# Two transformer layers on one core: fixed load order, free PSUM banks for the first projections, PV placed behind scores, and a new order table

## The chip, the cores and the metric

The kernel runs on one core of one Trainium2 chip. The metric is the device time of one launch in microseconds (us). The engines that appear below are PE (TensorE, matrix multiply; its weight loads are listed apart as PEld), DVE (VectorE), ACT (ScalarE), POOL (GpSimd) and SP (SyncE, which only issues DMA transfers here). Every engine runs its own list of instructions in the order in which the program wrote it and waits for others by semaphores.

## The reference

The input is x, one sequence of 2048 tokens with 512 channels in bf16. Two layers are computed with the same weights. Each layer is a sliding-window attention followed by an MLP, both with a layer norm in front and a residual behind:

```
x = x + A(layernorm(x));  x = x + B(layernorm(x))      # this line twice

A: q, k, v = split(x @ wqkv)                # 32 heads of 16 channels
   s = q k^T / 4;  s = -1e9 where not 0 <= i - j < 256
   o = softmax(s) v;  return o @ wo
B: return gelu_tanh(x @ w1 + b1) @ w2 + b2  # 512 -> 1792 -> 512
```

A query sees its own key and the 255 before it. The layer norm has neither scale nor shift.

## The kernel before

**Tiles and stages.** x stays in SBUF as 16 tiles of 128 tokens (`X`). Two layers make 32 tiles, taken as 16 blocks of two tiles (256 tokens). For a block b the stages are:

- `lnq(b)`: for each tile statistics (`bn_stats`, L635), `rstd` on POOL (L642), the normalized tile `xn` (L645), a PE transpose (L36) and its copy to `xnTA` (L622 on DVE or L624 on ACT); then the Q projection in two groups of 512 columns, each for two of the four 128-channel chunks.
- `kv(b)`: the K projection in two such groups, each copied by DVE with a parity mask into `KT` (L712), and the V projection, one group a tile, copied into `Va`.
- `attention(b)`: nine or ten *visits*. A visit is one group of 16 or 24 small score matmuls (32 x 64 tiles of the PE array, 8 of them side by side) into four PSUM banks, followed by two exponentials on ACT (L800, 128 x 1024 each) into the ring buffer `E`. Masks (L823, DVE or POOL) cut the window's edges.
- PV: for each half of the heads (cp = 0, 1) two *phases* of 32 to 64 small matmuls each (64 x 17 tiles) multiply `E` by `Va` into two banks. The column of ones in `Va` yields the sum for the softmax. DVE transposes (`TT`, L886), takes the reciprocal (`Rc`), multiplies (`TM`, L891) and transposes back (`OT`, L896).
- `outproj`: the output projection, the residual (L677) and the second layer norm into `xnTB`.
- `mlp(J)`: ten jobs of two or four tiles. Some of the first product's groups go over DVE (bias, L957) and a gelu in place on ACT (L960), the others straight through gelu on ACT (L970). The second product ends in the residual, and in the second layer in the DMA to the output.

All matrix multiplies of the projections and the MLP use the whole 128 x 128 array. Every matmul goes through L32 and every PE transpose through L36, whatever the stage, so in the trace the tiles' names tell them apart.

**What sets the order.** The order of each engine's instructions is written by a planner (`_Plan`) while the program is built. Each piece of work is a node with an engine, a duration in ns that the planner assumes, what it reads and writes, and a priority; a lower number goes first. `run` steps through time, and whenever an engine is free, it takes the ready node with the lowest priority, provided that a PSUM bank is to be had. Priorities come from the block (200 per block) plus offsets by stage, such as 16 per visit, 80 * cp + 95 for PV, 110 for the Q projection two blocks ahead and 140 for K and V of the next block. To each priority a step from an *order table* is added: two long strings `TUNE`, of which one character stands for one class of node. The first string gives a step of the character's code minus 80 (P is 0, a character is between about -46 and +46), the second leans a node to its other engine.

For each node the planner also assumes a fixed time until its result is visible, a 94 ns cost when PE goes from one tile shape to another (`SWITCH`), and 1300 ns for a change of ACT's function table. The shapes have the letters f (whole array), r (scores) and c (PV).

**PSUM.** Eight banks are shared by classes: `sc` (four banks for a visit), `o` (bank 6 or 7, for all projections and transposes), `od` (two banks for PV) and `m1` (any one bank, for the first MLP product).

**Loads.** SP issues twelve loads from one queue. `load` is called in the order x tiles 0-1, Wqkv part 0 (Q), part 1 (K), x tiles 2-3, Wqkv part 2 (V), b1, x tiles 4-7, Wo, b2, W1, x tiles 8-15, W2. It gives each a planned issue time `i`, 480 ns after the one before, and a priority made from it:

```
dma(fn, writes, prio=-1000.0 + i / 1e3, dur=sp_t[1] - i, issue=issue)
```

Then `add` puts the table's step on that priority as on any other. The issue lines are L595 (x), L600 (Wqkv), L609 (b1), L611 (Wo), L612 (b2), L613 (W1) and L615 (W2).

Of the kernel before, what the change touches and what calls it, by code (L numbers as in the profile page):

```python
# [180 lines left out]
class _Plan:  # L181
# [5 lines left out]
    AFF = 0.0  # L187
# [9 lines left out]
    def add(self, eng, fn, dur, reads=(), writes=(), prio=0.0, alloc=None, free=(), after=(), geo=None, table=None,  # L197
            dma=False, alt=(), war=(), lock=False, joins=()):
# [20 lines left out]
        if free and eng == "dve":  # L219
# [5 lines left out]
            alts=((eng, fn, dur, 0.0),) + alt, key=k, done=False, behind=None,  # L225
            heavy=any(a[0] == "pool" and a[2] > 600.0 for a in ((eng, fn, dur),) + alt),
        ))
        return i

    def run(self):  # L230
# [15 lines left out]
        last_lock = {"dve": None, "pool": None}  # L246
        last_geo = None
# [22 lines left out]
        seq = n  # L270
        while left:
# [9 lines left out]
            for e in engs:  # L281
                while pend[e] and pend[e][0][0] <= t + 1e-9:
                    _, i = heapq.heappop(pend[e])
                    for a in nodes[i]["alts"]:
                        if a[0] == e:
                            heapq.heappush(ready[e], (nodes[i]["prio"] + a[3], i))
                if efree[e] > t + 1e-9 or not ready[e]:
                    continue
                skipped = []
                pick = best = None  # L290
                while ready[e]:
                    p, i = heapq.heappop(ready[e])
                    nd = nodes[i]
                    if nd["done"]:
                        continue
                    if best is not None and p > best[0] + self.AFF:
                        skipped.append((p, i))
                        break
                    if (e == "pool" and locked["dve"] + (self.TAIL["dve"] + self.WAKE["pool"] if nd["heavy"] else 0.0) > t + 1e-9) or (
                            e == "dve" and nd["lock"] and locked["pool"] > t + 1e-9):  # L300
                        skipped.append((p, i))
                        continue
                    if nd["alloc"] is not None and fit(nd["alloc"][0]) is None:
                        skipped.append((p, i))
                        continue
                    if best is None:
                        best = (p, i)
                        pick = i
                        if e != "pe" or nd["geo"] == last_geo:
                            break  # L310
                    elif nd["geo"] == last_geo:
                        skipped.append(best)
                        pick = i
                        break
                    else:
                        skipped.append((p, i))
                for s in skipped:
                    if s[1] != pick:
                        heapq.heappush(ready[e], s)
                if pick is None:  # L320
                    continue
                nd = nodes[pick]
# [68 lines left out]
def bass_interleave_layers__sliding_block__dense_activation_gelu__prompt_kernel(  # L391
# [46 lines left out]
    PVLAG = 1  # L438
    POOL_M = 1110.0
# [19 lines left out]
    with ExitStack() as kctx:  # L459
        S_ = _Sched(nc, kctx)  # L460

        def sb(name, shape, dtype=dt.bfloat16):
# [73 lines left out]
        }, TUNE)  # L536
        add = PL.add

# [65 lines left out]
        load_x(0, 2)  # L604
        load_qkv(0)
        load_qkv(1)
        load_x(2, 2)
# [12 lines left out]
        def evac(dst, src, n, reads, writes, prio, free=(), after=(), two=False, kind="", boot=False):  # L620

            return add("dve", lambda e, B: e.tensor_copy(dst(B), src(B)), 334 if two else d_psum(n),  # L622
                       reads=reads, writes=writes + ([] if free else reads), prio=prio, free=free, after=after,
                       alt=() if kind not in ACT_OK and not boot else (("act", lambda e, B: e.activation(dst(B), src(B), AF.Copy, scale=1.0), d_act(n), 0.0 if boot else ACT_H),))  # L624
# [3 lines left out]
        def layernorm(tau, layer, dst, dcol, dname, prio):  # L628
# [21 lines left out]
            def tr(e, B):  # L650
# [5 lines left out]
                alloc=("o", [(g, 1)]), geo="f", war=[dname])  # L656
# [23 lines left out]
        def lnq(b, prio):  # L680

            xs = b % 2
            for j in range(2):
                layernorm(2 * b + j, 0, xnTA[:, xs], j * P, "xa%d_%d" % (xs, j), prio)
            xr = ["xa%d_0" % xs, "xa%d_1" % xs]
# [12 lines left out]
        def proj(g, which, i, xs, xr, prio, war):  # L698
            for half in range(2):
# [351 lines left out]
```

## Time and profile before

| what | value |
|---|---|
| median of 3 runs | 494.89 us (493.67 to 494.89) |
| the profiled execution, whole | 499.72 us |
| its span, first to last instruction | 498.0 us |
| mean granted PE clock | 0.976 |
| busy: PE / ACT / DVE / POOL | 459.2 / 403.6 / 370.4 / 217.3 us |
| PE matmuls | 8897 |
| exponentials (L800) | 304, 1032 ns each, 290.2 us |
| HBM read / written | 8.00 / 2.10 MB |

A row of the trace in order of time has the start in us, the duration in us, the engine, the line, the operation, the tile written and the tiles read, the shapes, the count of merged instructions, and in brackets the idle time before and what ended it. The rows of stretches give each engine's busy time with its number of instructions, then the granted clock, the share of the DMA engines and their rate. Matmuls overlap, and their ends are modelled, so distances between starts are safer than single durations.

### The profile page before, as it was taken

How to read it: one execution, taken by the hardware profiler on the slowest of the kernel's cores; microseconds unless marked ns; L12 is line 12 of the kernel's file. 1: busy time of each engine (PE TensorE's matmuls, PEld its weight loads, DVE VectorE, ACT ScalarE, POOL GpSimd, SP SyncE). 2: the span in 40 equal slices, each digit the busy share in tenths (PEclk: the TensorE clock that was granted, in tenths of full speed). 3: DMA queues.
4: the chain of work that ended last, by engine and by line, in shares of the span. 5: the costliest groups of instructions: out<-in, count | busy, mean ns of one | idle time of the engine just before them, and what ended most of it. 6: DMA issues, size and time to landing. Idle time of an engine off the chain costs nothing.

```text
span 498.0 us, 19388 instructions
## 1 busy us (share of the span) xinstructions
PE 459.2 (92%) x8897; PEld 245.5 (49%) x8897; DVE 370.4 (74%) x749; ACT 403.6 (81%) x481; POOL 217.3 (44%) x245
## 2 busy tenths in 40 slices
PE   4389769989988999999999999999998999999897
PEld 2254446465543545545544554455544444544554
DVE  4089887788997858987999689886887858773541
ACT  1079989889897889998899988899897899868433
POOL 4039772723655344644387306453342534630020
PEclk9599899999998999999999999999999999999899
DMA  7910000000000000000000000000000000100010
GB/s 235 364 45 3 3 4 3 3 3 1 4 3 3 3 2 5 3 3 3 3 3 3 3 3 3 4 2 3 13 13 24 3 9 8 34 1 24 12 33 21
DMA packets 9117, 11.33 MB, mean 23 GB/s; under 512 B 460, under 2 KB 8524, under 8 KB 9036
## 3 DMA queue, kind: packets, MB, share of 16 engines
q1 hardware_dynamic: 9036, 10.10, 6.2%
q8 instruction: 69, 1.13, 1.0%
q14 instruction: 12, 0.10, 0.1%
HBM read 8.00 MB, written 2.10 MB: 20 GB/s over the span
## 4 chain that ended last, share of the span: by engine, by line
PE 79%; DVE 9%; ACT 4%; SPq 3%; issue 2%; DMA 2%; POOL 0%; POOLq 0%
PE ps L32 76%; ACT E L800 3%; PE ps L36 2%; DMA Wqkv_sb<-in_A_wqkv_dram 2%; DVE KT L712 2%; SPq L595 2%; DVE stat L635 1%; DVE TT L886 1%; DVE Va L622 1%; SPq L600 1%; DVE X L677 1%; POOL E L823 0%; DVE xnTA L622 0%; DVE TM L891 0%; SPq L613 0%
## 5 line engine op out<-in xcount | busy, mean ns | idle before, releaser
L800 ACT ACTIVATE E<-ps 128x1024 bf16<-128x1024 f32 x304 | 290.2, 1032 | 28.3 <-PE ps L32 26.3
L823 POOL TENSOR_TENSOR E<-E,mask 128x512 bf16<-128x512 bf16 (+1 forms) x123 | 133.3, 1097 | 121.7 <-ACT E L800 57.9
L32 PE MATMUL ps<-W_sb,gT 128*128 128x512 bf16 x448 | 116.9, 384 | 0.0
L32 PE MATMUL ps<-xnTB,W_sb 128*128 128x512 bf16 (+1 forms) x560 | 110.9, 340 | 1.9 <-ACT xnTB L624 0.9
L642 POOL TENSOR_TENSOR rstd<-veps,mhalf 128x1 f32<-128x1 f32 x64 | 37.4, 596 | 108.9 <-DVE veps L639 108.6
L32 PE MATMUL ps<-xnTA,Wqkv_sb 128*128 128x256 bf16 x512 | 71.8, 283 | 13.0 <-DMA Wqkv_sb<-in_A_wqkv_dram 12.7
L32 PEld LDWEIGHTS ps<-xnTB,W_sb 128*128 128x128 bf16 x560 | 51.6, 98 | 44.2 <-issue 3.3
L32 PE MATMUL ps<-QT,KT 32*64 32x320 bf16 (+4 forms) x2976 | 66.7, 260 | 7.1 <-issue 3.9
L677 DVE TENSOR_TENSOR X<-X,ps 128x512 bf16<-128x512 bf16 x64 | 43.7, 683 | 35.9 <-PE ps L32 34.9
L970 ACT ACTIVATE gT<-ps,b1T 128x512 bf16<-128x512 f32 (+1 forms) x92 | 49.7, 586 | 20.0 <-PE ps L32 19.9
L823 DVE TENSOR_TENSOR E<-E,mask 128x512 bf16<-128x512 bf16 (+1 forms) x137 | 56.6, 439 | 12.3 <-ACT E L800 11.8
L32 PEld LDWEIGHTS ps<-xnTA,Wqkv_sb 128*128 128x128 bf16 x512 | 47.5, 101 | 33.5 <-issue 16.2
L32 PEld LDWEIGHTS ps<-W_sb,gT 128*128 128x128 bf16 x448 | 39.4, 98 | 44.7 <-issue 7.4
L712 DVE TENSOR_TENSOR KT<-ps,parmask 128x1024 bf16<-128x1024 f32 x32 | 38.8, 1219 | 25.6 <-PE ps L32 25.2
L32 PE MATMUL ps<-E,Va 64*17 64x192 bf16 (+3 forms) x3872 | 49.4, 230 | 7.5 <-issue 5.2
L32 PEld LDWEIGHTS ps<-QT,KT 32*64 32x64 bf16 x2976 | 28.0, 104 | 53.4 <-ACT E L800 34.1
L32 PEld LDWEIGHTS ps<-E,Va 64*17 64x17 bf16 x3872 | 39.4, 85 | 23.6 <-issue 10.0
L886 DVE STREAM_TRANSPOSE TT<-ps 128x1024 f32<-128x1024 f32 x32 | 39.8, 1245 | 14.1 <-PE ps L32 13.7
L635 DVE BATCH_NORM_STATS2 stat<-X 128x6 f32<-128x512 bf16 x64 | 43.4, 684 | 1.2 <-DMA X<-in_A_x_dram 0.5
L930 POOL TENSOR_TENSOR X<-X,b2b 128x512 bf16<-128x512 bf16 x32 | 36.6, 1153 | 17.4 <-DVE E L823 8.8
L957 DVE TENSOR_SCALAR gT<-ps,b1T 128x512 bf16<-128x512 f32 (+1 forms) x48 | 32.0, 674 | 7.5 <-PE ps L32 6.6
L32 PE MATMUL ps<-Wqkv_sb,xnTA 128*128 128x512 bf16 x128 | 33.5, 381 | 0.8 <-DMA Wqkv_sb<-in_A_wqkv_dram 0.7
(48 smaller groups left out, 335.6 us busy)
## 6 DMA issues: line engine op xcount, KB each, us to landing
W_sb<-in_B_w_dram SPq DMA_DIRECT2D x2, 1792.0 KB, 13.5
out_dram<-X SPq DMA_DIRECT2D x16, 128.0 KB, 1.7
Wqkv_sb<-in_A_wqkv_dram SPq DMA_DIRECT2D x3, 512.0 KB, 10.5
X<-in_A_x_dram SPq DMA_DIRECT2D x1, 1024.0 KB, 13.1
X<-in_A_x_dram SPq DMA_DIRECT2D x2, 256.0 KB, 2.9
X<-in_A_x_dram SPq DMA_DIRECT2D x1, 512.0 KB, 10.7
Wo_sb<-in_A_wo_dram SPq DMA_DIRECT2D x1, 512.0 KB, 8.8
b2b<-in_B_b_dram SPq DMA_DIRECT2D x1, 128.0 KB, 6.7
```

Of the source, the lines that this page charges most:

```text
L32: return self.e.matmul(*a, **k)
L36: return self.e.transpose(*a, **k)
L635: add("dve", lambda e, B: e.bn_stats(stat6[:, k6, :], X[:, t, :]), 590, reads=["X%d" % t], writes=["st%d" % k6], prio=prio)
L642: add("pool", lambda e, B: e.tensor_tensor(out=rstd[:, k : k + 1], in0=veps[:, k : k + 1], in1=mhalf[:], op=ALU.pow), 535, reads=["ve%d" % ...
L677: add("dve", lambda e, B: e.tensor_tensor(out=X[:, t, :], in0=X[:, t, :], in1=ps[:, B[g][0], :], op=ALU.add), d_psum(512), reads=["X%d" % ...
L712: add("dve", lambda e, B, g=g, i=i: e.tensor_tensor(out=KT[:, kb, :, 2 * i : 2 * i + 2, :].rearrange("p a c q -> p a (c q)"), in0=ps[:, B[ ...
L800: last_exp[0] = add("act", lambda e, B, g_=g_, gi=gi: e.activation(E[:, 2 * gi : 2 * gi + 2, e0 : e0 + 512], ps[:, B[g_][0] : B[g_][0] + 2 ...
L823: op = lambda e, B, Ew=Ew, Mw=Mw: e.tensor_tensor(out=Ew, in0=Ew, in1=Mw, op=ALU.mult)
L886: add("dve", lambda e, B: e.transpose(TT[:, s].rearrange("p a c q d -> p (a c q d)"), ps[:, B[g][0] : B[g][0] + 2, :].rearrange("p a n -> ...
L930: add("pool", lambda e, B: e.tensor_tensor(out=X[:, t, :], in0=X[:, t, :], in1=b2b[:], op=ALU.add), 1110, reads=["X%d" % t, "b2b"], writes ...
L957: add("dve", lambda e, B, g=g, fc=fc: e.tensor_scalar(out=gT[:, fc, 0:M], in0=ps[:, B[g][0], 0:M], scalar1=b1T[:, fc : fc + 1], scalar2=No ...
L970: gelu_last[0] = add("act", lambda e, B, g=g, fc=fc: e.activation(gT[:, fc, 0:M], ps[:, B[g][0], 0:M], AF.Gelu_apprx_tanh, bias=b1T[:, fc ...
```

## The change

**Loads.** `load` uses `-1e5 + i` as the priority, so the loads lie 480 apart. The call for x tiles 2-3 moves ahead of the Wqkv parts.

**First projections.** The Q projection of blocks 0 and 1, and K and V of block 0, take their PSUM bank from class `m1` instead of `o`; the transposes of the first four tiles do so as well. Their priorities go from -60..-30 to -900 (Q of block 0), -890 (K), -880 (Q of block 1) and -350 (V), and the second channel pair of Q and K gets 400 more than the first.

**The planner's choice for PE.** The rule that took a node of the same shape among equal priorities is gone. For PE every ready node's priority now gets an offset by the last shape and its own (`TURN`): +100 from f to c, +10 from f to r, -100 from r to c, -60 from c to r. An argument `chain`, which could hold a node behind another, is added, but no call uses it.

**Early offsets.** For blocks 0, 1 and 2 the output projection gets -100, -80 and -50, and PV half of that.

**Constants.** Planned durations: PV phase 638 ns instead of 640, and 344 instead of 472 for the first block of a layer; TT +36, the reciprocal 260 instead of 130, TM on POOL 1110 instead of 1200, OT 630 instead of 600, copies on ACT +14.

**Order table.** Both strings are replaced. The instructions themselves, their shapes and their number by stage stay; which engine takes a node that has two may change, and so may the order of all five engines. The loop inside a PV phase is rewritten with the same matmuls in the same order.

```diff
-                            heapq.heappush(ready[e], (nodes[i]["prio"] + a[3], i))
+                            if e == "pe":
+                                ready[e].append((nodes[i]["prio"] + a[3], i))
+                            else:
+                                heapq.heappush(ready[e], (nodes[i]["prio"] + a[3], i))
...
+                elif e == "pe":
+                    best = None
+                    for p, i in ready[e]:
+                        nd = nodes[i]
+                        if nd["done"] or nd["chained"] or (nd["alloc"] is not None and fit(nd["alloc"][0]) is None):
+                            continue
+                        x = (p + self.TURN.get((last_geo, nd["geo"]), 0.0), i)
+                        if best is None or x < best:
+                            best = x
+                    if best is not None:
+                        pick = best[1]
...
+    EARLY = {0: -100.0, 1: -80.0, 2: -50.0}
...
+        TURN = {("f", "c"): 100.0, ("f", "r"): 10.0, ("r", "c"): -100.0, ("c", "r"): -60.0}
...
-            dma(fn, writes, prio=-1000.0 + i / 1e3, dur=sp_t[1] - i, issue=issue)
+            dma(fn, writes, prio=-1e5 + i, dur=sp_t[1] - i, issue=issue)
...
         load_x(0, 2)
+        load_x(2, 2)
         load_qkv(0)
         load_qkv(1)
-        load_x(2, 2)
         load_qkv(2)
...
-                alloc=("o", [(g, 1)]), geo="f", war=[dname])
+                alloc=("m1" if tau < 4 and not layer else "o", [(g, 1)]), geo="f", war=[dname])
...
-                proj(g, 0, i, xs, xr, prio, ["Q%d_%d" % (cb, 2 * i + c) for cb in cols for c in range(2)])
+                prio = base + pair[i]
+                proj(g, 0, i, xs, xr, prio, ["Q%d_%d" % (cb, 2 * i + c) for cb in cols for c in range(2)], "m1" if b < 2 else "o")
...
-                pr = prio + 80 * cp + 95
+                pr = prio + 80 * cp + 95 + EARLY.get(b, 0.0) / 2
...
-                    add("pe", fn, 640.0 if t0 else 472.0, reads=rd, writes=["ps:" + g, "pv%d_%d_%d" % (b, cp, phase)], prio=pr,
+                    add("pe", fn, 638.0 if t0 else 344.0, reads=rd, writes=["ps:" + g, "pv%d_%d_%d" % (b, cp, phase)], prio=pr,
...
-            pr = prio + 20 * NV + 40
+            pr = prio + 20 * NV + 40 + EARLY.get(b, 0.0)
...
-        lnq(0, -60)
-        kv(0, -50, -30)
-        lnq(1, -55)
+        lnq(0, -900, (0, 400))
+        kv(0, -890, -350, (0, 400))
+        lnq(1, -880, (0, 400))
```

More of the change, by code (lines that the diff above doesn't have):

```diff
@@ L246, in run @@
         last_lock = {"dve": None, "pool": None}
+        held = {e: None for e in engs}
+        for nd in nodes:
+            nd["chained"] = False
+        for nd in nodes:
+            if nd["then"] is not None:
+                nodes[nd["then"]]["chained"] = True
         last_geo = None
@@ L291, in run @@
[L291 to L312, printed above, removed]
+                pick = None
@@ new lines, in run @@
+                if held[e] is not None:
+                    if (held[e] in [x[1] for x in ready[e]]):
+                        pick = held[e]
+                elif e == "pe":
[9 more added lines that the diff above has]
+                        pick = best[1]
+                else:
+                    skipped = []
+                    while ready[e]:
+                        p, i = heapq.heappop(ready[e])
+                        nd = nodes[i]
+                        if nd["done"]:
+                            continue
+                        if (e == "pool" and locked["dve"] + (self.TAIL["dve"] + self.WAKE["pool"] if nd["heavy"] else 0.0) > t + 1e-9) or (
+                                e == "dve" and nd["lock"] and locked["pool"] > t + 1e-9):
+                            skipped.append((p, i))
+                            continue
@@ L313, in run @@
                         pick = i
                         break
[L315 to L319, printed above, removed]
+                    for x in skipped:
+                        heapq.heappush(ready[e], x)
                 if pick is None:
                     continue
+                if e == "pe":
+                    ready[e] = [x for x in ready[e] if x[1] != pick and not nodes[x[1]]["done"]]
+                    held[e] = nodes[pick]["then"]
@@ L847, in pv @@
                 npi = max(len(q) for q in seq)
-                for phase in range(2):
+                steps = [(phase, c) for phase in range(2) for c in (2 * cp, 2 * cp + 1)]
+                need = []
+                for phase, c in steps:
                     rd = []
@@ L851, in pv @@
                         for k, q_lo, q_hi, e0 in seq[half]:
[L852 to L855 removed]
+                            pos, n, vn = moving(k, 2 * c + (half ^ phase), e0, (q_hi - q_lo) * HK)
+                            rd += ["E%d%s" % (ch, x) for ch in chunks(pos, n) for x in "abd"] + [vn]
@@ L881, in fn @@
-                        return x
-                    add("pe", fn, 640.0 if t0 else 472.0, reads=rd, writes=["ps:" + g, "pv%d_%d_%d" % (b, cp, phase)], prio=pr,
+                        for c, pi in [(c, pi) for c in (2 * cp, 2 * cp + 1) for pi in range(npi)]:
+                            for half in range(2):
+                                if pi >= len(seq[half]):
+                                    continue
+                                k, q_lo, q_hi, e0 = seq[half][pi]
+                                par = half ^ phase
+                                rows = slice(HK * half, HK * half + HK)
+                                pos, n, _ = moving(k, 2 * c + par, e0, (q_hi - q_lo) * HK)
+                                e1 = pos % RING
+                                o = (c - 2 * cp) * 256 + q_lo * HK
+                                last = phase == 1 and c % 2 == 1 and pi == len(seq[half]) - 1
+                                cuts = [(e1, o, n)] if e1 + n <= RING else [(e1, o, RING - e1), (0, o + RING - e1, n - RING + e1)]
+                                for x1, o1, n1 in cuts:
+                                    for r in range(RG):
+                                        x = e.matmul(
+                                            ps[32 * r : 32 * r + VW, B[g][par], o1 : o1 + n1],
+                                            Va[rows, (2 * b + k) % VR, c * HC + 2 * r + par, :],
+                                            E[rows, r, x1 : x1 + n1],
+                                            start=phase == 0 and (par, r) not in opened,
+                                            stop=last and (x1, o1, n1) == cuts[-1], skip_group_check=True)
+                                        opened.add((par, r))
```

126 lines of the change are left out of this document (54 added, 72 removed).

## The prediction

> **What bounds the kernel now.** I read the page first, then the table by stretches, then the start in order of time. The page says which engine is the bound over the whole run:
>
> ```profile
> PE 459.2 (92%) x8897; PEld 245.5 (49%) x8897; DVE 370.4 (74%) x749; ACT 403.6 (81%) x481; POOL 217.3 (44%) x245
> ...
> PE   4389769989988999999999999999998999999897
> ...
> PE 79%; DVE 9%; ACT 4%; SPq 3%; issue 2%; DMA 2%; POOL 0%; POOLq 0%
> ```
>
> PE is busy 459.2 of 498.0 us and holds 79% of the chain of waits. Its holes are in the first six slices. The stretches (columns: PE, PEld, DVE, ACT, POOL busy, granted clock, DMA share, GB/s) put numbers on them:
>
> ```profile
> 0.00:10.00 10.00, 6.08 (x24) 2.52 (x24) 5.75 (x19) 1.88 (x2) 5.60 (x22) 1.00 0.69 201
> 10.00:20.00 10.00, 0.01 (x1) 0.04 (x2) 0.08 (x1) 0.00 (x0) 0.00 (x0) 0.61 1.06 375
> 20.00:30.00 10.00, 8.65 (x52) 5.88 (x52) 4.66 (x15) 3.58 (x6) 1.42 (x3) 0.71 0.71 225
> ...
> 40.00:50.00 10.00, 8.80 (x197) 4.88 (x190) 10.00 (x26) 9.20 (x12) 10.00 (x13) 1.00 0.01 2
> 50.00:60.00 10.00, 7.60 (x200) 4.62 (x199) 8.92 (x16) 9.71 (x12) 7.98 (x9) 0.83 0.01 3
> 60.00:70.00 10.00, 7.32 (x237) 4.22 (x235) 9.21 (x20) 9.25 (x11) 6.91 (x8) 1.00 0.01 3
> 70.00:80.00 10.00, 8.34 (x168) 6.11 (x168) 7.43 (x15) 8.96 (x13) 5.63 (x5) 1.00 0.01 2
> ...
> 100.00:150.00 50.00, 45.63 (x1070) 26.83 (x1069) 43.11 (x86) 46.46 (x57) 23.04 (x24) 1.00 0.01 3
> ...
> 200.00:250.00 50.00, 49.87 (x1089) 26.61 (x1094) 43.38 (x91) 45.19 (x52) 24.44 (x29) 1.00 0.01 3
> ```
>
> There are three regimes. From 10 to 20 us every engine stands still while DMA runs at 375 GB/s. From 40 to 80 us ScalarE (9.2, 9.7, 9.3, 9.0 of 10) sets the pace and PE has holes. Later PE is full: 49.87 of 50 from 200 us on. The start in order of time says why nothing runs:
>
> ```profile
> 0.79 0.95 SPq L595 DMA_DIRECT2D X<-in_A_x_dram  x2
> ...
> 2.29 0.43 SPq L615 DMA_DIRECT2D W_sb<-in_B_w_dram  x1
> ...
> 2.76 1.67 SPq L613 DMA_DIRECT2D W_sb<-in_B_w_dram  x1
> ...
> 4.48 4.80 SPq L600 DMA_DIRECT2D Wqkv_sb<-in_A_wqkv_dram  x1
> ...
> 7.35 0.42 DVE L622 COPY xnTA<-ps 128x512 bf16<-128x512 bf16 x1
> ...
> 9.15 0.93 DVE L645 TENSOR_SCALAR xn<-X,statmv,rstd 128x512 bf16<-128x512 bf16 x2 [0.31 <-POOL rstd L642]
> ...
> 19.99 5.28 PE L32 MATMUL ps<-xnTA,Wqkv_sb 128*128 128x256 bf16 x24 [12.68 <-DMA Wqkv_sb<-in_A_wqkv_dram]
> ...
> 26.45 1.28 DVE L635 BATCH_NORM_STATS2 stat<-X 128x6 f32<-128x512 bf16 x2
> ...
> 28.31 1.91 PE L32 MATMUL ps<-xnTA,Wqkv_sb 128*128 128x256 bf16 x16
> ...
> 30.15 0.42 PE L32 MATMUL ps<-QT,KT 32*64 32x320 bf16 x16
> ...
> 30.75 1.94 ACT L800 ACTIVATE E<-ps 128x1024 bf16<-128x1024 f32 x2
> ```
>
> The two MLP weights (L613, L615) stand ahead of the first 512 KB of Wqkv. The order table did this: the loads differ by 0.48 in priority per issue, and a character of the table shifts a load by up to tens. The operand of the first projection is ready at 7.35 + 0.42 = 7.8 us; the projection starts at 19.99 and the first exponential at 30.75.
>
> **Loads and first projections.** The new load priorities lie 480 apart, so the table cannot reorder them: x tiles 0-1, 2-3, then the three parts of Wqkv. Nothing is added to the SP queue; twelve load issues stay twelve, only their places move. The two small x transfers are already first. The page has size and time to landing of each issue:
>
> ```profile
> W_sb<-in_B_w_dram SPq DMA_DIRECT2D x2, 1792.0 KB, 13.5
> ...
> Wqkv_sb<-in_A_wqkv_dram SPq DMA_DIRECT2D x3, 512.0 KB, 10.5
> ...
> X<-in_A_x_dram SPq DMA_DIRECT2D x2, 256.0 KB, 2.9
> ```
>
> They land 2.9 us after their issue. The second is issued by 1.28 us (halfway through the 0.95) and lands near 4.2. Behind it 512 KB take 1.4 us at 375 GB/s or 2.6 at the first stretch's 201 GB/s: Wqkv part 0 lands between 5.6 and 6.8, ahead of the operand. The far bound is the 10.5 us row taken whole from an issue at 1.8, which gives 12.3; that is a transfer behind a full queue, so I stay with the near end. PE then resumes at 7.9 instead of 20.0, **12.1 us** earlier (7.7 at the far bound).
>
> The 24 matmuls at 19.99 take 5.28/24 = 0.220 us each, the 16 at 28.31 take 1.91/16 = 0.119. The granted clock between is 0.61 and 0.71, so the long pause is paid twice; without it these 24 cost 24 x 0.101 = **2.4 us** less. The Trainium skill ("TensorE: Matmul & The Clock Gate", Part 1) says an idle window of about 3.4 us puts the clock back to half rate; the trace's 0.61 agrees, and by that rule this gain is lost only if the weights land after 10.7 us.
>
> Then comes the split of the first projections into pairs: channel chunks 0-1 of Q0, K0 and Q1 come first, chunks 2-3 (400 later) and V (-350) behind. Before the first scores stand 24 matmuls of 256 columns instead of 40 and a V group. They may use any of eight PSUM banks instead of two, so no projection waits for an evacuation. Q0 and K0 end at 7.9 + 16 x 0.119 = 9.8; xn of tiles 2-3 ends at 9.15 + 0.93 = 10.1; transposes, one copy (0.42 on DVE), eight matmuls (1.0) and a copy bring the first scores to about 12.9 us, against 30.15: **-17.2 us** for these three steps together. Bounds: 12.3 if the last copy overlaps the chunk before it, 17.3 if Wqkv lands at the far bound (4.4 later), so -18 to -13. W1 and W2 (1792 KB each) are late next, for they now stand behind everything but part of x. Even at 201 GB/s all loads (7.8 MB by their sizes) are in by 40 us, and the first MLP matmul comes far behind that, near 57 after the shift:
>
> ```profile
> 73.98 0.28 PE L32 MATMUL ps<-xnTB,W_sb 128*128 128x256 bf16 x1 [0.90 <-ACT xnTB L624]
> ```
>
> So this move costs nothing, with 17 us of cover.
>
> **What DVE gives back.** Between 26.45 and 30 us DVE did four bn_stats of later tiles (two take 1.28, so about 2.7 us, and 1.2 us of their small operations by my estimate) while PE prepared its scores. That cover goes. DVE then was 10.00 of 10 busy from 40 to 50, so up to 3.9 us can come back as late K, Q and xn. ScalarE may take the early copies and later windows have slack (7.43 at 70-80). Bounds 0 to +3.9; I take the middle, **+2 us**.
>
> **PV behind scores.** Whether a change of tile shape costs time is read here (PE in order of time, one group a row):
>
> ```profile
> 1.23 5.63 PE L32 MATMUL ps<-gT 128*128 128x512 bf16 x16 [1.23 <-DVE gT L572]
> ...
> 160.85 1.47 PE L32 MATMUL ps<-xnTB,W_sb 128*128 128x512 bf16 x6
> 162.24 0.42 PE L32 MATMUL ps<-QT,KT 32*64 32x192 bf16 x16
> ...
> 165.15 4.49 PE L32 MATMUL ps<-xnTB,W_sb 128*128 128x512 bf16 x20
> 169.47 0.81 PE L32 MATMUL ps<-Wo_sb,OT 128*128 128x512 bf16 x3
> ...
> 488.76 6.21 PE L32 MATMUL ps<-W_sb,gT 128*128 128x512 bf16 x28
> ```
>
> Twenty dense matmuls take 169.47 - 165.15 = 4.32, 0.216 each. Six should take 1.30, but the scores start 1.39 after them: 0.09 us a change. Counted from the first PE row to the last (1.23 and 488.76), shapes change 396 times; 61 PV groups, of which only 10 come right behind scores and 39 stand alone between dense groups. The new offsets (dense to PV +100, scores to PV -100) make PE take PV after a visit. One change saved for each of the 39 is **-3.7 us**. The far end is -6, if each of 64 phases (two for each of 32 PV groups of banks) saves one; the other end 0, if PV waits for a visit and the TT transpose, OT and output projection behind it are late. PE has the dense queue as cover there. The PV durations in the planner move no work by themselves.
>
> This move puts more small instructions together, and the trace has a price for that:
>
> ```profile
> 376.06 0.80 PE L32 MATMUL ps<-E,Va 64*17 64x256 bf16 x64
> 376.79 0.40 PE L36 MATMUL ps<-ident,xn 128*128 128x128 bf16 x4
> 377.12 0.80 PE L32 MATMUL ps<-E,Va 64*17 64x256 bf16 x64
> 377.85 0.37 PE L32 MATMUL ps<-QT,KT 32*64 32x64 bf16 x15
> 379.70 0.37 PE L32 MATMUL ps<-QT,KT 32*64 32x320 bf16 x9 [1.48 <-issue]
> ```
>
> The waits in total (us, times, longest) and the page's instruction queue:
>
> ```profile
> PE ps L32 <- issue: 9.4, 8, 2.0
> ```
>
> ```profile
> q8 instruction: 69, 1.13, 1.0%
> ```
>
> After 147 matmuls with their weight loads (294 instructions in 2.2 us) PE stops 1.48 us inside a visit and waits for nothing but its own issue. Eight such pauses make 9.4 us. The 69 instruction packets match 2 x 8897 / 69 = 258 instructions each, so I read them as instruction fetch overtaken by a burst. A visit with one PV phase is (24 + 64) x 2 = 176 instructions, under 258, when dense work follows, which the zero offset after PV allows; both phases and two visits exceed it. I take **0**, with bounds -8 (all gone) and +8 (twice as many). The Trainium skill ("Runtime: NRT & Kernel Launch", Instruction fetch mechanics) calls crossing a 16 KiB boundary "mostly hidden"; by it this term and the slower rival below would be nothing, but the row contradicts it.
>
> **Earlier output projections, order table, constants.** Blocks 0-2 get PV 50, 40, 25 and output projections 100, 80, 50 earlier, so the first MLP starts sooner inside the stretch that ScalarE bounds. PE has 2.4 + 2.7 + 1.7 = 6.7 us of holes from 50 to 80; ScalarE is full there and gelu is its work too, so I count **-2 us** (0 to -5). The new table reorders everything else: from 200 us nothing is left to win, from 100 to 150 there are 4.4 us. I take 0, bounds -4 to +4.
>
> **Sum.** -17.2 + 2 - 3.7 + 0 - 2 + 0 = -20.9 us. The profiled execution took 499.7 us (span 498.0 and 1.7 around it, which nothing here touches), so 478.8 for its like; the median is 494.89, 4.8 less, so **about 474 us**.
>
> **Rivals.**
> - The start is won and partly lost again: DVE and ScalarE stay backed up to 80 us. For it: 10.00 and 9.20 of 10 at 40-50. Against: PE work, not DVE, fills the later 400 us. The 12.7 of the DMA wait are won, 3.9 come back in DVE and the holes of 50-80 grow by about 1: 494.9 - 7.8 = 487.
> - The plan fits the chip better throughout: pauses gone (-8), holes at 100-150 gone (-4). 474 - 12 = 462. For: the old plan assumed weights 13 us early. Against: PE is full from 200 on.
> - Slower: instruction fetch. At 1.6 us a pause, (between 1.48 and the longest, 2.0), the 20.9 us are eaten by 13 further pauses. If a pause hits one in three of the 64 PV phases, that is 21 pauses, 34 us, and 474 + 34 = 508. For: each long pause in the trace ends such a burst. Against: bursts of single phases stay under 258.
> - The loads do not come in the written order, or land no sooner: then the 12.7 us wait remains and only the shape changes and the fill, about 5 us, are left, near 490. Against: steps of 480 cannot be crossed by a character.
>
> **How the numbers follow.** Chances: forecast 0.62 (own range 467 to 482), start partly lost 0.15, better throughout 0.14, fetch pauses 0.05, loads not moved 0.04. Low 462 takes in about half of the better case, high 488 most of the partly lost one. Within 0.3% (1.5 us, about what a measurement can tell from no change) and slower come only from the fetch case and a fetch case mixed with loads that don't move: faster 0.93, same 0.02, slower 0.05.
>
> **What would show it.** The wait of 12.68 us for Wqkv should be gone; PE should resume by 9 us and the first L800 row stand near 13. The 10-20 stretch should show PE above 7 of 10 at clock 1.00. Groups of PV should follow scores, and "issue" before PE stay near 9 us. A first exponential after 18 us, or 20 us of issue pauses, would make the forecast wrong; so would PE holes of over 10 us between 30 and 80.

## The result, and the profile after

| | before | changed |
|---|---|---|
| median | 494.89 us (4 runs, 493.67 to 495.25) | 483.35 us (4 runs, 481.85 to 484.32) |
| ratio | | 0.977, 95% interval 0.974 to 0.980 |
| profiled span | 498.0 us | 482.6 us |

The change makes the kernel 11.5 us faster. The forecast was 474, 20.9 us faster: the direction and the range hold, the gain is little more than half of the one forecast. In the medians below, two of six runs of the loads alone and one of six of their repeat with x 8-15 moved up are left out, because they fell into a slower state of the chip.

The page of the changed kernel:

```profile
PE 446.3 (92%) x8807; PEld 246.2 (51%) x8897; DVE 367.3 (76%) x747; ACT 405.1 (84%) x481; POOL 221.6 (46%) x249
...
PE   8987899998889999999999999999999999999897
...
PEclk9997799999989999999999999999999999999999
...
PE 75%; DVE 9%; ACT 9%; issue 4%; DMA 1%; SPq 0%
```

The empty second slice is gone. The trace has 8807 of 8897 matmuls, so 90 records are missing. I read the many idle times of 0.16 us "issue" before a single dense matmul as such gaps: PE waits for issue 49 times here and 8 times in the first profile of before, which has every record. So busy PE can't be compared with before to a few us. The start in order of time, as it was shown of before:

```profile
0.78 0.95 SPq L611 DMA_DIRECT2D X<-in_A_x_dram  x2
...
1.78 1.56 SPq L616 DMA_DIRECT2D Wqkv_sb<-in_A_wqkv_dram  x3
...
8.45 0.23 PE L36 MATMUL ps<-ident,xn 128*128 128x128 bf16 x1 [0.60 <-DMA Wqkv_sb<-in_A_wqkv_dram]
...
9.20 0.83 PE L32 MATMUL ps<-xnTA,Wqkv_sb 128*128 128x256 bf16 x6 [0.52 <-DVE xnTA L638]
...
10.31 4.75 PE L32 MATMUL ps<-xnTA,Wqkv_sb 128*128 128x256 bf16 x42
...
15.11 1.67 PE L32 MATMUL ps<-Wqkv_sb,xnTA 128*128 128x512 bf16 x7
...
16.71 0.42 PE L32 MATMUL ps<-QT,KT 32*64 32x320 bf16 x16
...
17.32 2.90 ACT L821 ACTIVATE E<-ps 128x1024 bf16<-128x1024 f32 x3
```

The projections start at 9.20 us instead of 19.99, the scores at 16.71 instead of 30.15, the exponentials at 17.32 instead of 30.75. Ahead of the scores stand all 48 matmuls of 256 columns (6 and 42) and V, not 24. The stretches (columns as before) show where PE still has holes:

```profile
10.00:20.00 10.00, 9.78 (x113) 6.58 (x112) 8.86 (x23) 6.17 (x9) 2.13 (x4) 1.00 1.06 371
20.00:30.00 10.00, 8.51 (x152) 5.34 (x152) 8.97 (x25) 10.00 (x13) 6.18 (x7) 1.00 0.56 178
30.00:40.00 10.00, 7.50 (x207) 3.74 (x210) 9.63 (x23) 8.99 (x11) 10.00 (x11) 1.00 0.01 2
40.00:50.00 10.00, 9.15 (x179) 4.99 (x153) 7.83 (x14) 8.27 (x10) 6.29 (x9) 0.66 0.01 3
50.00:60.00 10.00, 7.81 (x228) 4.60 (x233) 7.02 (x17) 8.80 (x10) 7.07 (x8) 0.72 0.02 5
```

The 304 exponentials are the same in every version and come in the same order, so three times split each run: to the first exponential, from it to the start of the last, and from there to the end of the span. The first and the last start stand in the answer for the line of the exponential. Of the changed kernel (span 482.6):

```profile
L821 ACT ACTIVATE E<-ps x304: 1017/1024/1117, 17.3 to 441.8; 128x1024 bf16<-128x1024 f32 x152
```

Of the kernel before, profiled a second time (span 493.6, time 495.3 us, so nearer to its median than the first profile):

```profile
L800 ACT ACTIVATE E<-ps x304: 1018/1023/1138, 30.1 to 454.8; 128x1024 bf16<-128x1024 f32 x152
```

| profiled execution | to the first | first to last | last to end | span |
|---|---|---|---|---|
| before, first profile | 30.7 | 426.4 | 40.9 | 498.0 |
| before, second profile | 30.1 | 424.7 | 38.8 | 493.6 |
| changed | 17.3 | 424.5 | 40.8 | 482.6 |
| changed, second profile | 17.4 | 422.1 | 40.6 | 480.1 |

Against the second profile of before the start gives 12.8 us, the long middle 0.2, and the end takes 2.0 back. So the gain lies ahead of the first exponential; the middle differs by 2.4 us between the two profiles of the changed kernel alone.

### The profile page after: what moved, and what is told of

It is laid out like the page before. It is cut to its first block, busy times and chain, and to the rows that moved or that the text cites. A ratio compares the mean times of both kernels' runs of the same rounds, so it can differ in the third digit from the quotient of the medians.

```text
span 482.6 us, 19304 instructions
## 1 busy us (share of the span) xinstructions
PE 446.3 (92%) x8807; PEld 246.2 (51%) x8897; DVE 367.3 (76%) x747; ACT 405.1 (84%) x481; POOL 221.6 (46%) x249
## 4 chain that ended last, share of the span: by engine, by line
PE 75%; DVE 9%; ACT 9%; issue 4%; DMA 1%; SPq 0%
PE ps L32 72%; ACT E L821 6%; PE ps L36 3%; DVE KT L732 2%; ACT gT L993 2%; DVE stat L651 1%; DMA Wqkv_sb<-in_A_wqkv_dram 1%; DVE OT L919 1%; DVE gT L980 1%; DVE QT L638 1%; DVE X L693 1%; ACT gT L983 1%; DVE E L844 0%; DVE xnTA L638 0%; ACT Va L640 0%
## 5 line engine op out<-in xcount | busy, mean ns | idle before, releaser
L32 PE MATMUL ps<-W_sb,gT 128*128 128x512 bf16 x406 | 106.1, 380 | 4.4 <-issue 3.0
L32 PE MATMUL ps<-xnTB,W_sb 128*128 128x512 bf16 (+1 forms) x536 | 105.4, 336 | 4.2 <-issue 1.9
L32 PE MATMUL ps<-QT,KT 32*64 32x320 bf16 (+4 forms) x2976 | 67.4, 263 | 8.4 <-ACT E L821 4.2
L32 PEld LDWEIGHTS ps<-xnTB,W_sb 128*128 128x128 bf16 x560 | 51.5, 98 | 43.8 <-issue 3.6
L32 PE MATMUL ps<-xnTA,Wqkv_sb 128*128 128x256 bf16 x512 | 70.1, 281 | 1.5 <-DVE xnTA L638 0.8
L32 PEld LDWEIGHTS ps<-W_sb,gT 128*128 128x128 bf16 x448 | 39.9, 98 | 44.9 <-issue 5.4
L32 PE MATMUL ps<-E,Va 64*17 64x192 bf16 (+3 forms) x3872 | 50.3, 233 | 7.7 <-issue 3.7
L32 PEld LDWEIGHTS ps<-xnTA,Wqkv_sb 128*128 128x128 bf16 x512 | 47.7, 100 | 18.5 <-issue 3.2
L32 PEld LDWEIGHTS ps<-QT,KT 32*64 32x64 bf16 x2976 | 27.8, 104 | 56.9 <-ACT E L821 36.4
L32 PEld LDWEIGHTS ps<-E,Va 64*17 64x17 bf16 x3872 | 40.1, 86 | 22.0 <-issue 7.4
L32 PE MATMUL ps<-Wo_sb,OT 128*128 128x512 bf16 x120 | 30.9, 380 | 1.1 <-issue 0.6
```

The costliest lines, as they stand in the source:

```text
L32: return self.e.matmul(*a, **k)
```

## The experiments

**The loads alone, and the loads undone.** The kernel before keeps the planned order of PE, ACT, DVE and POOL; only the SP queue is rearranged behind the planner.

```diff
         order = PL.run()
+        first_loads = ["X0", "X2", "Wqkv0", "Wqkv1", "Wqkv2", "b1raw", "X4", "Wo", "b2b", "W1", "X8", "W2"]
+        sp_loads = {PL.nodes[i]["writes"][0]: i for i in order if PL.nodes[i]["eng"] == "sp" and not PL.nodes[i]["deps"]}
+        order = [sp_loads[n] for n in first_loads] + [i for i in order if i not in sp_loads.values()]
```

> The kernel before, with the order of PE, ACT, DVE and POOL exactly as its planner wrote it; only the twelve loads on the SP queue are put into the order of the changed kernel (x 0-3, three parts of Wqkv, b1, x 4-7, Wo, b2, W1, x 8-15, W2). Theory 1 (the whole gain is the start, and it comes from the loads alone): first exponential near 16 to 17.5 us instead of 30.75, every later part unchanged, median 480 to 484. Theory 2 (banks, PV rule and order table carry a good part): median 487 to 491.

The changed kernel gets the old order of loads by the same lines with

```diff
+        first_loads = ["X0", "X2", "b2b", "W2", "W1", "Wqkv0", "b1raw", "Wqkv1", "X8", "X4", "Wqkv2", "Wo"]
```

> The changed kernel with all its orders as planned, but the twelve loads on the SP queue in the order that the kernel before had (x 0-3, b2, W2, W1, Wqkv 0, b1, Wqkv 1, x 8-15, x 4-7, Wqkv 2, Wo). Theory 1: the gain is gone, first exponential at 29 to 32 us, median 493 to 499. Theory 2: 486 to 490, still clearly under the kernel before.

Measured: the loads alone take 482.9 us, ratio to before 0.971 (0.966 to 0.977), against 0.977 for the whole change. With the loads undone the change takes 496.6, ratio 1.002 (0.999 to 1.006). Theory 1 holds on both sides: the loads carry the whole gain, and everything else of the change is in sum worth nothing beside them. In the trace of the loads alone (span 481.4) the first exponential is earlier than in the changed kernel, and earlier than the 16 to 17.5 us expected, but the middle is longer:

```profile
L800 ACT ACTIVATE E<-ps x304: 1018/1023/1098, 15.1 to 442.5; 128x1024 bf16<-128x1024 f32 x152
```

442.5 - 15.1 = 427.4 against 424.7. In order of time, DVE, PE and ACT show the place:

```profile
22.64 0.69 DVE L635 BATCH_NORM_STATS2 stat<-X 128x6 f32<-128x512 bf16 x1 [2.94 <-DMA X<-in_A_x_dram]
23.25 0.67 DVE L622 CAST QT<-ps 128x512 bf16<-128x512 f32 x1
...
23.98 1.09 PE L32 MATMUL ps<-xnTA,Wqkv_sb 128*128 128x256 bf16 x8 [2.80 <-DVE QT L622]
...
25.72 1.94 ACT L800 ACTIVATE E<-ps 128x1024 bf16<-128x1024 f32 x2 [2.86 <-PE ps L32]
```

The old order of DVE reads x 8-15 early, because the old queue had it early; in the written order it comes behind W1 and lands at 22.6 us. Behind the waiting instruction stands a copy of Q; PE waits for that copy, ACT for PE.

**The kernel before, profiled again.**

> The kernel before, unchanged, profiled once more. Its first profile lasted 499.7 us against a median of 494.9. If the extra 4.8 us lie in the wait for the first weights, the first exponential comes near 26 us here with a time of 494 to 496; if they lie elsewhere (clock, fetch pauses), it stays at 30 to 31 and the rest is shorter.

495.3 us, first exponential at 30.1. So the extra time of the first profile was not the wait for weights. Of the 4.4 us between the spans 0.6 lie at the start. Most of the rest are pauses of PE over 0.3 us, 9.4 us in the first profile and 6.7 in the second; seven of the eight stand at the same instructions in both and last differently. The rows behind the two longest, of the first profile:

```profile
151.16 0.36 PE L32 MATMUL ps<-E,Va 64*17 64x192 bf16 x24 [2.00 <-issue]
...
462.37 0.50 PE L32 MATMUL ps<-E,Va 64*17 64x64 bf16 x37 [1.81 <-issue]
```

and of the second:

```profile
148.74 0.48 PE L32 MATMUL ps<-E,Va 64*17 64x192 bf16 x24 [0.91 <-issue]
...
459.62 0.49 PE L32 MATMUL ps<-E,Va 64*17 64x64 bf16 x37 [1.29 <-issue]
```

**The first projections really deferred.**

```diff
-        lnq(0, -900, (0, 400))
-        kv(0, -890, -350, (0, 400))
-        lnq(1, -880, (0, 400))
+        lnq(0, -900, (0, 940))
+        kv(0, -890, 50, (0, 940))
+        lnq(1, -880, (0, 950))
```

> The changed kernel, with the second channel pair of the first Q and K groups 940 to 950 behind the first instead of 400, and the first V at 50 instead of -350, so that they really stand behind the first visit in priority; everything is planned again with the same order table. First exponential expected near 13.5 to 14.5 us against 17.3. If what is won at the first exponential is kept to the end: median 479 to 481. If the later order, for which the table was not made, takes it back: 485 to 493.

490.7 us, ratio 0.987 (0.982 to 0.991). The first exponential came at 14.9, 2.4 us earlier than in the changed kernel, and the run was longer, by 7.3 us between the medians and by some 5 by the ratios: the second expectation. From first to last exponential it took 431.8 us instead of 424.5. The start of PE:

```profile
9.39 0.23 PE L36 MATMUL ps<-ident,xn 128*128 128x128 bf16 x1 [1.18 <-DMA Wqkv_sb<-in_A_wqkv_dram]
...
10.14 0.83 PE L32 MATMUL ps<-xnTA,Wqkv_sb 128*128 128x256 bf16 x6 [0.52 <-DVE xnTA L638]
...
11.26 2.13 PE L32 MATMUL ps<-xnTA,Wqkv_sb 128*128 128x256 bf16 x18
13.44 1.03 PE L32 MATMUL ps<-Wqkv_sb,xnTA 128*128 128x512 bf16 x4
14.39 0.42 PE L32 MATMUL ps<-QT,KT 32*64 32x320 bf16 x16
```

Five changed priorities let the planner write the queues anew: DVE has 738 instructions instead of 747, ACT 488 instead of 481. That the table, made for another order, no longer fits is my reading; which step of the later order costs the time was not looked for. Here what was won ahead of the first exponential was not kept to the end; in the next run, in which every queue but that of the loads is unchanged, it was.

**x 8-15 ahead of the weights.** The loads alone, with one place changed:

```diff
-        first_loads = ["X0", "X2", "Wqkv0", "Wqkv1", "Wqkv2", "b1raw", "X4", "Wo", "b2b", "W1", "X8", "W2"]
+        first_loads = ["X0", "X2", "Wqkv0", "Wqkv1", "Wqkv2", "b1raw", "X4", "X8", "Wo", "b2b", "W1", "W2"]
```

> As the run with the loads alone (the orders of the kernel before on PE, ACT, DVE and POOL), but with x 8-15 moved up in the SP queue, right behind x 4-7 and ahead of Wo, b2, W1 and W2. In that run DVE waited 2.94 us at 22.6 us for x 8-15, behind it the copy of Q, PE 2.80 us and ACT 2.86 us. Theory (that wait was on the path and all of it is kept to the end): the wait is gone, median 2.5 to 3.5 us under the run with the loads alone. Rival (the stretch to 80 us is bound by DVE and ACT anyway, and the time comes back): within 1.5 us of it.

480.4 us, ratio 0.970 (0.966 to 0.974); 2.5 us under the loads alone by the medians, the near edge of the expected 2.5 to 3.5. The intervals of the two ratios overlap, so the time alone doesn't settle it; the trace does (span 478.6):

```profile
L800 ACT ACTIVATE E<-ps x304: 1017/1024/1092, 15.4 to 439.8; 128x1024 bf16<-128x1024 f32 x152
```

From first to last exponential 424.4 us instead of 427.4: the 3 us are back and kept to the end. This is the kernel before with nothing but twelve loads in another order. It was put beside the changed kernel on one chip:

> The changed kernel again, to stand on the same chip beside the next run. If the place of x 8-15 is worth what the two earlier runs say, and the changed kernel is not better than the old orders with the loads alone: 482.5 to 485, some 3 us more than the next run. If they are equal: within 1.5 us.

> The orders of the kernel before with the loads in the written order and x 8-15 right behind x 4-7, again: 479.5 to 482, under the changed kernel by about 3 us; the rival is a tie within 1.5 us.

The changed kernel 484.6 us, ratio 0.978 (0.975 to 0.981); the old orders with this queue 479.6, ratio 0.970 (0.966 to 0.975). The medians differ by 5.0 us, more than expected, and the intervals just touch. It came out the same way twice. The two profiled executions differ by less, 480.1 against 477.8 of span:

```profile
L821 ACT ACTIVATE E<-ps x304: 1018/1023/1125, 17.4 to 439.5; 128x1024 bf16<-128x1024 f32 x152
```

```profile
L800 ACT ACTIVATE E<-ps x304: 1018/1023/1138, 15.2 to 439.0; 128x1024 bf16<-128x1024 f32 x152
```

The first exponential comes 2.2 us later in the changed kernel, the middle is 1.7 shorter (422.1 against 423.8), and behind the last exponential stand 1.8 us more (40.6 against 38.8). There the new order has four PV phases in one burst and pauses in it:

```profile
441.56 2.31 PE L32 MATMUL ps<-E,Va 64*17 64x256 bf16 x224
445.72 0.47 PE L32 MATMUL ps<-E,Va 64*17 64x256 bf16 x32 [1.85 <-issue]
```

The pause is not the difference, for the old order pauses in the same four phases:

```profile
442.04 0.45 PE L32 MATMUL ps<-E,Va 64*17 64x256 bf16 x27 [0.25 <-PE ps L32]
443.83 0.49 PE L32 MATMUL ps<-E,Va 64*17 64x64 bf16 x37 [1.34 <-issue]
```

With three shorter gaps beside it (0.25, 0.25 and 0.16 us) that is about as much as 1.85. What differs is work: by the weight loads, which have no missing records, 87 matmuls of the second MLP product and 16 transposes stand behind the last scores instead of 82 and 8. At 0.22 us for such a matmul the five make 1.1 us, and the rest of the 1.8 is about what the transposes take.

**More changes of tile shape.** In the changed kernel each PV phase is cut where dense pieces follow it, and the pieces alternate (`fs`, at most four of them; 23 cuts; PE's written order has 444 changes of shape instead of 398). No matmul is added.

```diff
+            fs = fs[:-1]
...
+            cut = [cnt.n * j // (len(fs) + 1) for j in range(len(fs) + 2)]
...
+        order = [x for i in order for x in ([i, after_f[i]] if i in after_f else [i])]
```

> The changed kernel with all its orders, only that PV phases are cut into pieces between which the dense pieces that follow them are put, 23 cuts, which makes 46 more changes of tile shape with the same matmuls. Theory (0.09 us a change, on the path): 4.1 us more than the changed kernel, and in the trace 0.09 us at each change. Rival (a change costs nothing when other work is late anyway): no more than 1.5 us.

488.3 us, ratio 0.986 (0.981 to 0.990). Against the two measurements of the changed kernel (0.977 and 0.978) that is 0.008 to 0.009 of 495, or 3.8 to 4.4 us for 46 changes: 0.08 to 0.10 us each. The intervals of the ratios leave this sum uncertain by some 3 us either way, and in the profiled execution the first exponential came 1.0 to 1.1 us later (18.4): K's weights landed 7.2 us after their issue instead of 6.1 or 6.2, which the cuts don't touch. The trace gives the price more closely where one phase stands whole and the next one cut:

```profile
93.40 0.80 PE L32 MATMUL ps<-E,Va 64*17 64x256 bf16 x64
94.13 0.39 PE L32 MATMUL ps<-xnTA,Wqkv_sb 128*128 128x256 bf16 x2
94.45 0.47 PE L32 MATMUL ps<-E,Va 64*17 64x256 bf16 x32
94.85 0.28 PE L32 MATMUL ps<-xnTB,W_sb 128*128 128x256 bf16 x1
95.06 0.46 PE L32 MATMUL ps<-E,Va 64*17 64x256 bf16 x32
95.46 3.56 PE L32 MATMUL ps<-xnTB,W_sb 128*128 128x256 bf16 x31
```

Whole: 94.13 - 93.40 = 0.73 us. In halves: 0.40 and 0.40, and one dense matmul takes 0.21, where 31 of them take 98.85 - 95.46 = 3.39, 0.11 each. Two changes cost 0.07 + 0.10 = 0.17.

**What is left without a table.** Four kernels with an empty order table and the loads in the written order:

```diff
+        TUNE = ("", "")
```

> The changed kernel with an empty order table: no step on any priority, all its rules (offsets by shape, early offsets, banks, constants) as they are. Beside it stands the kernel before with an empty table and the loads in the written order. Theory 3 (the rules of the change make a better order of their own, the tables are worth more than both): this one 500 to 510, and 5 to 10 us under the other. Rival (rules are worth nothing without a table made for them): the two within 3 us of each other.

> The kernel before with an empty order table, its load priorities 480 apart and x 2-3 ahead of Wqkv as in the changed kernel; no offsets by shape, no early offsets, projections in banks 6 and 7. Theory 3: 506 to 516, above the changed kernel without a table by 5 to 10 us. Rival: within 3 us of it.

Measured 501.5 and 513.7 us, ratios 1.011 (1.007 to 1.015) and 1.036 (1.032 to 1.040): theory 3, with a difference of 12.2 us, over the 5 to 10 expected. Each table is worth more than the load order: 18 us the new one (501.5 to 483.4), 31 us the old one (513.7 to 482.9, the loads alone). Without tables the changed rules are 12.2 us better; with them that difference is gone. Two further kernels take the rules apart. The first drops the offsets by shape:

```diff
-        TURN = {("f", "c"): 100.0, ("f", "r"): 10.0, ("r", "c"): -100.0, ("c", "r"): -60.0}
+        TURN = {}
```

> The changed kernel with an empty order table and with no offsets by shape (TURN empty; the early offsets then change nothing in the order, for every PE node is taken at its bare priority). Between the two kernels without a table lie 12.2 us (501.5 and 513.7). Theory 4 (the offsets by shape are what makes the difference): 508 to 514. Rival (it is the order and the banks of the first projections and the planner's constants): 500 to 504.

500.0 us, ratio 1.010 (1.006 to 1.014): theory 4 falls, the offsets by shape are worth no measurable time here either. (The early offsets are part of the priorities themselves, so, other than the expectation says, they still act in this kernel and in the next.) The second also gives the first projections their old priorities and banks 6 and 7:

```diff
-        lnq(0, -900, (0, 400))
-        kv(0, -890, -350, (0, 400))
-        lnq(1, -880, (0, 400))
+        lnq(0, -60)
+        kv(0, -50, -30)
+        lnq(1, -55)
```

> As the changed kernel without table and without offsets by shape (500.0), and its first projections also go back to the priorities (-60 to -30) and the two banks of the kernel before. What is left of the change beside the load order are the planner's constants and the plain choice by priority on PE. If the new first projections make the 12 us between the two kernels without a table: 510 to 514. If the constants and the choice make them: 498 to 502.

502.1 us, ratio 1.012 (1.008 to 1.017): within the intervals of the one before. What is left, 502.1 against 513.7, are the planner's constants, the early offsets and the way PE's next piece is chosen; which of the three, and whether another order without a table would show the same, stays open, since each is one plan.

## Why the prediction was right or wrong

**The load order** was the mechanism, as forecast, and without it nothing remains (496.6). The two MLP weights ahead of Wqkv were read rightly, and the time lies where the chain of waits had it. The landing was forecast well, and the first reader was not. The Q part, issued at 1.78, landed 5.1 us later, at 6.9; I had taken 6.8 as the later end. But the new order of PE takes K first, whose copy stands ahead of every copy of Q, and the K part is second in the queue: issued at 2.29, it landed 6.1 us later, at 8.4.

```profile
DMA to landing us min/median/max: 5.1/6.1/7.1
```

```profile
10.85 1.22 DVE L732 TENSOR_TENSOR KT<-ps,parmask 128x1024 bf16<-128x1024 f32 x1
...
12.26 0.60 ACT L640 ACTIVATE QT<-ps 128x512 bf16<-128x512 f32 x1 [1.37 <-PE ps L32]
```

A transpose carries that wait until 8.45, 0.60 us of it idle, and the projections start at 9.20 instead of 7.9. The loads alone, with the old order of PE, which takes Q first, start at 7.70.

**"Before the first scores stand 24 matmuls of 256 columns instead of 40 and a V group"** is the step that failed. All 48 and the V matmuls stand there. I read 400 and -350 as places behind the scores, but -900 + 400 = -500 and -350 are still ahead of the first visit's priority, which is 0 and up; a number in a priority says nothing until it stands beside its rival. The 24 more take some 24 x 4.75/42 = 2.7 us and V 1.7 (rows at 10.31 and 15.11). Scores came at 16.71 instead of 12.9. That is inside the bound of 17.3, but by luck: the bound was made for weights that land late. With the projections really deferred the scores stand at 14.39, 4.25 us behind the first projection instead of 7.51, although one V group is still ahead of them: the misplaced work cost 3.3 us. The term of -17.2 measured -13.4.

**DVE gives back 2 us.** Not seen in the changed kernel: 424.5 us and 422.1 from first to last exponential against 424.7. In the loads alone 2.7 were given back, by a load that DVE's order met too early. I had looked only at who needs W1 and W2, and not at x 8-15, whose place among the loads moves as well.

**PV behind scores, -3.7.** The price was right (0.09 us forecast, 0.08 to 0.10 measured), the count was not. In the written order of PE, counted by the weight loads, shapes change 398 times instead of 396, and PV follows scores 8 times instead of 10. An offset only helps a piece that is ready when the scores end. A PV phase also needs its last masked exponentials, and its second phase waits for the first; such a pair stands in the trace as before:

```profile
65.94 0.80 PE L32 MATMUL ps<-E,Va 64*17 64x256 bf16 x64
66.67 0.39 PE L32 MATMUL ps<-xnTB,W_sb 128*128 128x256 bf16 x2
67.00 0.80 PE L32 MATMUL ps<-E,Va 64*17 64x256 bf16 x64
```

That readiness is the cause was argued from the code and this row, not tested, and it is not all: without a table the same offsets do bring PV behind scores 16 times instead of 5, with 385 changes of shape instead of 403, so the steps of the new table have a part in the 8. And 18 changes fewer, 1.6 us at 0.09, did not show in the time (501.5 with the offsets, 500.0 without).

**Fetch pauses, 0** held in sum. The pauses over 0.3 us make 9.4 and 6.7 us in the two profiles of before, 6.9 and 7.6 in those of the changed kernel. The wait total ("PE ps L32 <- issue") isn't the measure here, since it counts the missing matmul records too. The rival with 13 more pauses didn't come: PV and scores weren't packed together. That the pauses are instruction fetch stays a reading from the packet count; no run tests it. Eight pauses stand against 69 instruction packets, so most packets cost no pause that the trace shows, and "the row contradicts it" holds for the eight alone.

**Earlier output projections, -2** brought nothing: the first MLP matmul stands at 61.63, 44.3 us after the first exponential, against 73.98 - 30.75 = 43.2 before.

**Order table, 0** can't be told apart from the other rules: together they are worth nothing in sum (496.6 with the loads undone). I had not seen what the 0 stands for: the two tables bring two sets of rules, 12.2 us apart without them, to about the same time.

**The sum** from the second profile of before: -12.8 at the start, -0.2 in the middle, +2.0 at the end, -11.0 of span, against -11.5 of the medians. Of the 9.9 us that are missing against the forecast of -20.9, the start has 4.4 and the end 2.0. The other 3.5 are the middle, where -3.7 (PV), -2 (output projections) and +2 (DVE) were forecast and -0.2 came. The rival "the start is won and partly lost again", 487, was nearer in size, but its cause isn't the one found: the middle, in which DVE's and ACT's backlog to 80 us would show, is no longer than before.

## What to carry to other kernels

When an order is searched or planned, first see in the trace whether the plan's assumptions hold on the chip: here twelve loads in the wrong places cost 13 to 16 us, and repairing them behind the planner, with every other queue untouched, gave as much as a new plan, and with one place changed some 3 to 5 us more. When a transfer moves in a queue, or the order of a reader changes, look for each engine's first reader of every transfer, not only of the large ones: DVE met x 8-15 too early, and the new order of PE met K's weights ahead of Q's. A priority offset must be compared with the priorities that it is to pass, and it does nothing for work that isn't ready.

## What the runs showed of the hardware that was not expected

- In the changed kernel the granted PE clock fell to half although PE had no long idle time. By stretches of 4 us (columns as above):

```profile
36.00:40.00 4.00, 1.94 (x68) 1.12 (x69) 3.63 (x11) 4.00 (x6) 4.00 (x6) 1.00 0.00 0
40.00:44.00 4.00, 3.51 (x111) 1.87 (x84) 3.29 (x7) 3.79 (x5) 2.26 (x4) 0.58 0.02 4
...
52.00:56.00 4.00, 2.40 (x120) 1.57 (x128) 2.79 (x9) 4.00 (x6) 3.68 (x5) 0.79 0.03 8
56.00:60.00 4.00, 3.84 (x98) 2.27 (x90) 2.23 (x4) 2.80 (x4) 1.39 (x3) 0.50 0.01 4
```

The longest single wait of PE from 25 to 60 us:

```profile
PE ps L32 <- DVE E L844: 1.1, 1, 1.1
```

A stretch in which PE was busy 1.94 or 2.40 of 4 us, in pieces, was followed by one at 0.58 or 0.50. "TensorE: Matmul & The Clock Gate" in the Trainium skill, Part 1, ties the drop to an idle window of about 3.4 us, and also tells of a kernel whose clock went back and forth because PE idled briefly but often between groups of matmuls. The rows here look like the second. It does not happen each time: in the second profile of the same kernel the granted clock from 40 to 60 was 0.83 and 1.00, against 0.66 and 0.72, and a stretch with PE busy 2.44 of 4 us from 52 was followed by one at 1.00. That profile's middle is 2.4 us shorter; that the clock is the cause is not shown.

- The pauses of PE in dense bursts mostly come at the same instructions in both executions of an order (seven of eight in the kernel before, seven of eight in the changed one), but one of them lasted 2.00 us in one and 0.91 in another, and one of 1.11 us came in one execution of the changed kernel alone.
- What an order costs is large beside these effects: the tables are worth 18 and 31 us on the same work, and five altered priorities under an unaltered table lost 5 to 7. The table of the changed kernel did not serve a slightly altered set of rules.
